# Order and queue of two kinds of loads in the last stage of an FNet and GEGLU kernel

## The chip, the core and the metric

The kernel runs on one core of a Trainium2 chip. The core has a matrix engine (TensorE, PE in the profile), a vector engine (VectorE, DVE), a scalar engine (ScalarE, ACT), a general engine (GpSimd, POOL) and an engine that mostly issues transfers (SyncE, SP). The engines run side by side, each through its own instructions in order, and wait for each other by semaphores. SBUF is the on-chip memory of 128 partitions, PSUM the small memory that TensorE adds into, and the large memory outside is called DRAM in the code. Transfers between DRAM and SBUF are DMAs. SyncE, ScalarE and GpSimd can issue them; each has a queue of its own, and the 16 DMA engines serve all queues.

The metric is device time in microseconds of one execution. Lower is better.

## The reference

`x` has 2048 rows of 448. It is layer-normalised to `xn`. One branch takes the real part of a two-dimensional discrete Fourier transform, with matrices given as inputs; the other is a gated feed-forward network:

```python
a = xn @ hid_re.T;  b = xn @ hid_im.T              # 2048 x 448 each
s = seq_re @ a - seq_im @ b                        # 2048 x 2048 times 2048 x 448
g = silu((gelu(xn @ w_gate) * (xn @ w_up)) @ w_down)
out = x + s * g
```

## The kernel before

All numbers are float32. TensorE works on a rounded form of them (`fp32r`, one pass); where more precision is needed a number is split into a high part, which is the rounded value, and a low part, which is the rest. ScalarE writes the high part and VectorE subtracts it from the number to get the low part (`split`, lines 118 to 120: line 119 is ScalarE's copy, line 120 VectorE's subtraction).

The kernel first computes the feed-forward branch (until about 410 us), then `a` and `b` (`hid_mm`, until about 491 us), and last the product with the 2048 x 2048 matrices, which this change touches. In the last stage the 16 blocks of 128 output rows are taken two at a time: eight rounds, `j` = 0 to 7. The 16 blocks `k` of the inner dimension are taken one after the other. Fourteen of them (`KS`) go through a scheme in the manner of Strassen's multiplication, with seven products where plain multiplication has eight (`seven`); the other two (`KP`) are multiplied plainly, once for each of the two row blocks ("t0" and "t1", `plain`). A round so has 16 units. TensorE takes some 2.2 us for each.

For every one of the fourteen blocks there is a **row tile**: `a` and `b` of that block in seven combinations (blocks 0 to 6 of 448 columns, in which 224 high numbers are followed by their 224 low parts). In the order of `PRODUCTS`, a unit's seven products read the blocks 0, 5, 2, 3, 4, 6 and 1 of its row tile. A product is two matmuls: line 975 multiplies the high part of a coefficient piece with the whole block, line 978 its low part with the block's high half.

Fourteen row tiles do not all fit into SBUF. Ten stay there (`KR`). Of the four others (blocks 0, 1, 4 and 5) two at a time are in the tiles `ts_u0` and `ts_u1`; all four are written once to DRAM (`td`, line 844, by GpSimd). A round begins with the two that are there, goes through the ten, and ends with the two others, which by then have been loaded over the first two; the next round begins with these (`order`). These are the **kept row tiles**. Their loads (line 1042) are four DMAs a tile, each a quarter of the 3136 columns, 392 KB, issued by SyncE at the units 2 to 9 of a round (in the last round at 2, 2, 3 and so on to 8). They are used at the units 12 and 13, the last of the fourteen. In the last round the units 12 and 13 run together, each product for both tiles.

Each unit also needs its **coefficient piece**: combinations of four 128 x 128 blocks of the two matrices. Two DMAs bring it (`load_c`, lines 870 to 882): 192 KB of `ct`, which is input data (line 881), and 128 KB of `sums`, which the kernel has put together earlier in DRAM by an adding DMA (line 882). The plain units load 256 KB of `cp` instead (line 879). Five places hold pieces (`raw_at`; by turns parts of `raw`, `f` and, in the first round, `cc`). VectorE makes two more combinations from both halves of the piece (`sum_c`, lines 888 and 889), then the piece is split into high and low parts (`prep_c`). Both are written into the unit's four slots in turn.

The order of the work is written out by hand: while unit m of TensorE is issued, the combinations of unit m + 4 are made, unit m + 3 is split, and the load of unit m + 8 is issued into the place that m + 3 leaves. At the end of a round VectorE adds up the seven products from PSUM (`gather`, lines 998 to 1006), then in the next round multiplies by the other branch (loaded at line 961) and GpSimd adds `x` with an adding DMA (`give`, lines 1009 to 1019; line 1015). SyncE stores the result (line 1017).

In the built program the DMAs of SyncE use eight completion semaphores in turn, and a DMA waits until the one that used its semaphore before has landed. GpSimd's DMAs have eight of their own.

Of the kernel before, what the change touches and what calls it, by code (L numbers as in the profile page):

```python
# [8 lines left out]
F32 = mybir.dt.float32  # L9
# [4 lines left out]
P = 128  # L14
S = 2048
D = 448
# [15 lines left out]
KX = ((4, 5), (0, 1))  # L32
KP = (10, 15)
KS = sorted(KR + KX[0] + KX[1])
# [11 lines left out]
def fnet_geglu(ctx: ExitStack, tc: tile.TileContext, x, ca, ct, cp, et, wgu, wd, out):  # L46
# [13 lines left out]
    nc = tc.nc  # L60
# [37 lines left out]
    def bank(i, name):  # L98
        return psum.tile([P, 512], F32, name=name, tag=f"b{i}")
# [321 lines left out]
    with tc.manual_schedule():  # L421
# [201 lines left out]
        sums = [dram.tile([P, NS, 2 * P], F32, name=f"sums{j}") for j in range(NK // 2)]  # L623
# [119 lines left out]
        td = {k: dram.tile([P, 7 * D], F32, name=f"td{k}") for k in KX[0] + KX[1]}  # L743
# [8 lines left out]
        T7 = 7 * D  # L752
# [35 lines left out]
        TS, ab, behind = {}, {}, []  # L788
# [64 lines left out]
        def raw_at(m):  # L853
            if m in (4, 5, 9, 10):
                return cc[:, 896 * ((m + 1) % 5) :][:, :896]
            i = (2, 0, 1, 2, 0, 0, 0, 1, 2)[m] if m < 9 else (m - 11) % 5
            return a_r[:, 896 * i :][:, :896] if i < 3 else new["d0"][:, 896 * (i - 3) :][:, :896]
# [12 lines left out]
        def load_c(m):  # L870
            v = raw_at(m)
            if m >= len(units):

                if m < len(units) + 2:
                    nc.sync.dma_start(v[:, :D], xv[:, NK - 2 + m - len(units), :D])
                return
            j, k = units[m]
            if isinstance(k, str):
                nc.sync.dma_start(v[:, : 4 * P], cp[2 * j + int(k[1])])
            else:  # L880
                nc.sync.dma_start(v[:, : 3 * P], ct[j, :, KS.index(k)])
                nc.sync.dma_start(v[:, 4 * P : 6 * P], sums[j][:, KS.index(k)])

        def sum_c(m):

            if m < len(units) and not isinstance(units[m][1], str):
                _, cr1, ci1, s2, s1, _, s4 = [raw_at(m)[:, i * P : (i + 1) * P] for i in range(7)]
                nc.vector.tensor_add(s2, cr1, s1)  # L888
                nc.vector.tensor_add(s4, s2, ci1)  # L889
# [3 lines left out]
        def prep_c(m):  # L893

            if m >= len(units):
                return
            n = (4 if isinstance(units[m][1], str) else 7) * P
            h, l = [v[:, :n] for v in slot_at(m)]
            split(h, l, raw_at(m)[:, :n])
            c_hl[m] = h, l  # L900
            n = nxt.get(m, m + 5)
            if n:
                load_c(n)

        for k in [*range(14), 15, 14]:
# [26 lines left out]
            if k == 8:  # L932
                load_c(0)
# [3 lines left out]
            if k == 12:  # L937
                load_c(1)
                load_c(2)
                sum_c(3)  # L940
# [18 lines left out]
        def load_gx(j, t):  # L959
            if 2 * j + t < NK:  # L960
                nc.sync.dma_start(gx[t], gv[:, 2 * j + t])
# [2 lines left out]
        LOAD_AT = 2  # L964
        STORE_AT = 5, 8
        GX_AT = 11, 12
        PRODUCTS = {1: (1, 0), 6: (3, 5), 2: (2, 2), 7: (5, 3), 5: (4, 4), 3: (6, 6), 4: (0, 1)}

        def seven(m, ps, n=1):

            for q, (i, b) in PRODUCTS.items():
                for u in range(m, m + n):
                    v = TS[units[u][1]][:, b * D : (b + 1) * D]
                    h, l = [w[:, i * P : (i + 1) * P] for w in c_hl[u]]
                    nc.tensor.matmul(  # L975
                        ps[q][:, :D], h, v, start=u % UN == 0, stop=False, skip_group_check=True
                    )
                    nc.tensor.matmul(  # L978
                        ps[q][:, :HD], l, v[:, :HD],
                        start=False, stop=u % UN == NS - 1, skip_group_check=True,  # L980
                    )

        def plain(m, py):
            h, l = c_hl.pop(m)
            for i, k in enumerate(KP):
                for r in range(2):
                    vh, vl = ab[k][r]
                    o = (2 * i + r) * P
                    a, b = h[:, o : o + P], l[:, o : o + P]
                    nc.tensor.matmul(py[:, :D], a, vh, start=i + r == 0, stop=False)  # L990
                    nc.tensor.matmul(py[:, :D], a, vl, start=False, stop=False)
                    nc.tensor.matmul(py[:, :D], b, vh, start=False, stop=i + r == 2)
# [30 lines left out]
        for m, (j, k) in enumerate(units):  # L1023
            u = m % UN
            if u == 0:
                ps = {q: bank(banks[i], f"p{q}_{j}") for i, q in enumerate(PRODUCTS)}
            if u < NS:
                if j < NK // 2 - 1 or u < NS - 2:
                    seven(m, ps)
                elif u == NS - 2:  # L1030

                    seven(m, ps, 2)

                over = 8 if j < NK // 2 - 1 else 7
                for i in range(8):
                    if u != LOAD_AT + i * over // 8:
                        continue
                    i, h = divmod(i, 4)
                    TS[KX[(j + 1) % 2][i]] = TS[KX[j % 2][i]]
                    n, w = KX[(j + 1) % 2][i], T7 // 4  # L1040
                    part_ = slice(h * w, (h + 1) * w)
                    nc.sync.dma_start(TS[n][:, part_].bitcast(F32), td[n][:, part_])
            else:
                py = bank(banks[7 if u == NS else 0], f"py{u - NS}_{j}")
                plain(m, py)
            if u in GX_AT:
                load_gx(j, GX_AT.index(u))

            if u == NS + 1 and m < len(units) - 1:
                todo.pop()()  # L1050
            if m:
                sum_c(m + 4)
            if u == NS - 2 and j == NK // 2 - 1:
                prep_c(m + 3)
                todo = gather(ps)
                todo.insert(6, lambda: nc.vector.tensor_add(cs[0][0], cs[0][0], cs[0][1]))
                for f in todo:
                    f()
            elif u == NS - 1 and j == NK // 2 - 1:
                pass  # L1060
            elif u == NS - 1:
                todo = gather(ps)
                for f in todo[:3]:
                    f()
                prep_c(m + 3)
            elif u == NS:
                for f in todo[3:] if j < NK // 2 - 1 else ():
                    f()
                prep_c(m + 3)
                c = cs[0][0]  # L1070
                todo = [lambda c=c, py=py: nc.vector.tensor_add(c, c, py[:, :D])]
            elif m == len(units) - 1:
                x_ = [raw_at(m + 1 + t)[:, :D] for t in range(2)]
                y = raw_at(m + 3)[:, :D]
                c1, c0 = cs[1][0], cs[0][0]
                nc.vector.tensor_add(c1, c1, cs[1][1])
                todo.pop()()
                for c, t in ((c1, 1), (c0, 0)):
                    nc.vector.tensor_mul(c, c, gx[t])
                for c, t in ((c1, 1), (c0, 0)):  # L1080
                    nc.vector.tensor_add(c, c, x_[t])
                nc.sync.dma_start(ov[:, NK - 2], c0)
                halves = slice(0, HD), slice(HD, D)
                for e in halves:
                    nc.vector.tensor_mul(y[:, e], gx[1][:, e], py[:, e])
                for e, eng in zip(halves, (nc.sync, nc.scalar)):
                    nc.vector.tensor_add(c1[:, e], c1[:, e], y[:, e])
                    eng.dma_start(ov[:, NK - 1, e], c1[:, e])
            elif u == NS + 1:
                prep_c(m + 3)  # L1090
                c = cs[1][0]
                spare = give(j, 0)
                spare.append(lambda c=c, py=py: nc.vector.tensor_add(c, c, py[:, :D]))
                spare += give(j, 1)
                banks = banks[1:] + banks[:1]
            else:
                if m:
                    prep_c(m + 3)
                if m == 4:
                    sums14()  # L1100
                if m == 6:
                    hid_split(14)()
                    load_c(14)
                    load_c(15)
                if spare:
                    spare.pop(0)()
                if u in STORE_AT and stores:
                    stores.pop(0)()
# [57 lines left out]
```

## Time and profile before

| | us |
|---|---|
| median of 3 runs | 786.89 (786.73 to 787.07) |
| profiled execution, its own time | 785.82 |
| its span, first to last instruction | 783.9 |
| TensorE busy in the span | 774.9 (99%) |
| VectorE busy | 593.7 (76%) |
| ScalarE busy | 308.9 (39%) |
| GpSimd busy | 51.8 (7%) |

The profile is of one execution. Rows in order of time show the start in us from the beginning of the span, the duration in us, the engine (SPq is SyncE's DMA issue), the line of the kernel, the operation and the tiles (written <- read, numbers left out). A bracket at the end shows how long the engine was idle before and what ended this. Starts of TensorE's matmuls follow each other closer than their durations, since they are pipelined. Rows of stretches of time show the stretch, its length, the busy time of PE, PEld (TensorE's weight loads), DVE, ACT and POOL with their counts, then TensorE's granted clock, the DMA engines' busy share and GB/s. Rows of waits show who waited for whom: the total in us, how often, and the longest. Rows of groups show count, busy time, mean ns of one, and the idle time before them. Rows of DMA issues show the tiles, the queue, the count, KB each and the median us from issue to landing.

### The profile page before, as it was taken

The page shows a single profiled execution, that of the slowest core. Times are in us where ns is not written, and L with a number is a line of the kernel's source. Part 1 is how long each engine was busy: PE and PEld are TensorE (multiplying, and loading weights), DVE is VectorE, ACT ScalarE, POOL GpSimd, SP SyncE. Part 2 cuts the span into 40 slices and gives each one's busy share as a digit, 9 for nine tenths or more (in the row PEclk, how much of TensorE's full clock was granted, in tenths as well). Part 3 has the DMA queues.
Part 4 walks back from the last instruction along what each step waited for, and adds up shares of the span by engine and source line. Part 5 has one row for each costly group of instructions (what it writes and reads, how often), then busy time and mean ns, then how long its engine had stood idle before and what let it go on. Part 6 is the DMA issues. An engine that isn't in the chain of part 4 may idle for free.

```text
span 783.9 us, 11188 instructions
## 1 busy us (share of the span) xinstructions
PE 774.9 (99%) x4092; PEld 695.4 (89%) x4092; DVE 593.7 (76%) x1045; ACT 308.9 (39%) x430; POOL 51.8 (7%) x82
## 2 busy tenths in 40 slices
PE   9999999999999999999999999999999999999997
PEld 7888888888888888888889999999999999999996
DVE  7877876767766776776675676888888796969686
ACT  3874432331332322322232864544343444444341
POOL 1000211110110010100000000000000000000000
PEclk9999999999999999999999999999999999999999
DMA  8000575353292360546101651778796959697794
GB/s 319 25 3 25 167 220 117 121 121 117 48 258 55 121 135 10 161 131 158 34 13 52 254 229 51 239 256 277 245 318 212 350 172 367 198 322 231 279 278 166
DMA packets 62007, 134.37 MB, mean 171 GB/s; under 512 B 6784, under 2 KB 43520, under 8 KB 61056
## 3 DMA queue, kind: packets, MB, share of 16 engines
q1 hardware_dynamic: 56912, 109.22, 39.7%
q0 software_dynamic: 4896, 24.32, 14.2%
q8 instruction: 32, 0.52, 0.3%
q14 instruction: 23, 0.19, 0.1%
q10 hardware_dynamic: 144, 0.11, 0.0%
HBM read 119.87 MB, written 43.12 MB: 208 GB/s over the span
## 4 chain that ended last, share of the span: by engine, by line
PE 73%; DMA 12%; DVE 10%; issue 2%; SPq 1%; ACT 0%; DVEq 0%
PE x L346 23%; PE po L326 17%; PE ab L803 9%; PE p L975 8%; PE x L354 6%; PE p L978 4%; PE gu L276 4%; DMA ts_u<-td 3%; DMA out<-cc 3%; DVE xt L120 3%; DVE w L120 2%; DMA f<-sums 2%; DMA raw<-sums 2%; DMA raw<-ct 1%; DMA raw<-wgu 1%
## 5 line engine op out<-in xcount | busy, mean ns | idle before, releaser
L326 PE MATMUL po<-wd,hs 128*128 128x448 f32 x672 | 153.0, 366 | 0.0
L326 PEld LDWEIGHTS po<-wd,hs 128*128 128x128 f32 x672 | 125.7, 188 | 14.4
L346 PE MATMUL x<-xt,w 128*128 128x512 f32 x504 | 135.0, 391 | 0.0
L346 PEld LDWEIGHTS x<-xt,w 128*128 128x128 f32 x504 | 94.6, 188 | 16.9
L335 DVE TENSOR_TENSOR gacc<-gacc,po 128x448 f32<-128x448 f32 x96 | 59.1, 618 | 60.9 <-PE po L326 60.9
L119 ACT ACTIVATE w<-raw 128x896 fp32r<-128x896 f32 (+1 forms) x61 | 55.3, 908 | 72.6 <-DVE raw L889 33.7
L346 PE MATMUL x<-thl,w 128*128 128x512 f32 x288 | 77.5, 391 | 0.3 <-DVE tmp L406 0.3
L803 PE MATMUL ab<-w,xt 128*128 128x448 f32 x256 | 68.0, 365 | 0.0
L346 PEld LDWEIGHTS x<-thl,w 128*128 128x128 f32 x288 | 54.0, 188 | 11.6 <-DVE tmp L406 0.7
L354 PE MATMUL x<-xt,w 128*128 128x512 f32 x192 | 59.2, 390 | 0.0
L975 PE MATMUL p<-xt,w 128*128 128x448 f32 x168 | 54.1, 374 | 0.0
L401 ACT ACTIVATE hs<-tmp 128x512 fp32r<-128x512 f32 x24 | 15.2, 634 | 95.3 <-DVE tmp L399 95.3
L803 PEld LDWEIGHTS ab<-w,xt 128*128 128x128 f32 x256 | 48.1, 188 | 3.8
L386 ACT ACTIVATE tmp<-x 128x512 f32<-128x512 f32 x24 | 14.4, 599 | 89.4 <-PE x L354 89.4
L119 ACT ACTIVATE w<-f 128x896 fp32r<-128x896 f32 (+1 forms) x34 | 30.3, 891 | 48.0 <-DVE f L889 26.8
L120 DVE TENSOR_TENSOR w<-raw,w 128x896 fp32r<-128x896 f32 (+1 forms) x41 | 43.0, 1048 | 4.1 <-ACT w L119 3.6
L354 PEld LDWEIGHTS x<-xt,w 128*128 128x128 f32 x192 | 36.0, 188 | 7.7
L975 PE MATMUL p<-ts_u,w 128*128 128x448 f32 x112 | 37.3, 379 | 1.7 <-DMA ts_u<-td 0.7
L975 PE MATMUL p<-ts_u,ts_tmp 128*128 128x448 f32 x112 | 36.5, 374 | 0.0
L888 DVE TENSOR_TENSOR raw<-raw 128x128 f32<-128x128 f32 x69 | 19.9, 288 | 21.2 <-DMA raw<-sums 21.2
L975 PE MATMUL p<-hs,w 128*128 128x448 f32 x112 | 35.6, 374 | 0.0
L803 PE MATMUL ab<-wd,xt 128*128 128x448 f32 x96 | 35.1, 365 | 0.0
(234 smaller groups left out, 1600.0 us busy)
## 6 DMA issues: line engine op xcount, KB each, us to landing
ts_u<-td SPq DMA_DIRECT2D x64, 392.0 KB, 5.9
sums<-ca SPq DMA_DIRECT2D x16, 896.0 KB, 7.5
sums<-ca POOLq DMA_DIRECT2D x16, 896.0 KB, 9.5
raw<-ct SPq DMA_DIRECT2D x69, 192.0 KB, 4.5
raw<-sums SPq DMA_DIRECT2D x69, 128.0 KB, 4.5
f<-ct SPq DMA_DIRECT2D x39, 192.0 KB, 4.4
raw<-wgu SPq DMA_DIRECT2D x14, 512.0 KB, 4.2
td<-ts_u POOLq DMA_DIRECT2D x4, 1568.0 KB, 6.6
```

Source lines behind the costliest of these rows:

```text
L119: nc.scalar.activation(h, src, AF.Copy)
L120: nc.vector.tensor_sub(l, src, h)
L276: nc.tensor.matmul(ps[:, cols], a, xt[:, k, cols], start=n == 0, stop=n == len(mm) - 1)
L326: nc.tensor.matmul(po[:, :D], hs[:, a, kk * P : (kk + 1) * P], wdn[:, b, i], start=n == 0, stop=n == 5,)
L335: nc.vector.tensor_add(ga, ga, po[:, :D])
L346: nc.tensor.matmul(ps, a[i], b[j], start=first and n == 0, stop=n == 2, skip_group_check=True)
L354: nc.tensor.matmul(ps, w["k3" + "gu"[g]][0], xt[:, 3], start=False, stop=True, skip_group_check=True)
L401: nc.scalar.activation(hs[:, 0], g1, AF.Copy)
L803: nc.tensor.matmul(p[:, :D], a, b, start=n == 0, stop=n == len(mm) - 1)
L888: nc.vector.tensor_add(s2, cr1, s1)
L975: nc.tensor.matmul(ps[q][:, :D], h, v, start=u % UN == 0, stop=False, skip_group_check=True)
L978: nc.tensor.matmul(ps[q][:, :HD], l, v[:, :HD], start=False, stop=u % UN == NS - 1, skip_group_check=True,)
```

## The change

Two things change, both in the loads of the last stage.

First, the four parts in which a kept row tile is loaded are no longer quarters of its columns. They are blocks 0 and 5, blocks 2 and 3, blocks 4 and 6, and block 1: the order in which the products of a unit read them. Three parts have two blocks (448 KB), the last has one (224 KB). They are issued by SyncE at the same units as before.

Second, the `sums` half of each coefficient piece is issued by GpSimd and no longer by SyncE. These are 112 DMAs of 128 KB. The `ct` half stays with SyncE.

```diff
@@ load_c
                 nc.sync.dma_start(v[:, : 3 * P], ct[j, :, KS.index(k)])
-                nc.sync.dma_start(v[:, 4 * P : 6 * P], sums[j][:, KS.index(k)])
+                nc.gpsimd.dma_start(v[:, 4 * P : 6 * P], sums[j][:, KS.index(k)])
@@ last stage
+        PARTS = slice(0, 6, 5), slice(2, 4), slice(4, 7, 2), slice(1, 2)
         PRODUCTS = {1: (1, 0), 6: (3, 5), 2: (2, 2), 7: (5, 3), 5: (4, 4), 3: (6, 6), 4: (0, 1)}
@@ in the loop over the units
                     TS[KX[(j + 1) % 2][i]] = TS[KX[j % 2][i]]
-                    n, w = KX[(j + 1) % 2][i], T7 // 4
-                    part_ = slice(h * w, (h + 1) * w)
-                    nc.sync.dma_start(TS[n][:, part_].bitcast(F32), td[n][:, part_])
+                    n = KX[(j + 1) % 2][i]
+                    a, b = [v.rearrange("p (b d) -> p b d", d=D) for v in (TS[n], td[n])]
+                    a, b = a[:, PARTS[h]], b[:, PARTS[h]]
+                    nc.sync.dma_start(a.bitcast(F32), b)
```

## The prediction

> **What bounds the kernel now.** I read the page's first part, then the busy time by stretch, then TensorE's instructions in order of time at the places where it was idle, and last the issues and landings of the DMAs ahead of those places.
>
> ```profile
> PE 774.9 (99%) x4092; PEld 695.4 (89%) x4092; DVE 593.7 (76%) x1045; ACT 308.9 (39%) x430; POOL 51.8 (7%) x82
> ```
>
> TensorE is the bound: 774.9 of 783.9 us. A change that leaves its instructions alone can only remove idle time or add some. The diff touches loads of the last stage alone, so only that stage's idle time is at stake. Five rounds of the last stage (a round is 16 units, about 36 us) give this sum over their stretches:
>
> ```profile
> sum 180.00, PE 178.66 PEld 168.63 DVE 148.21 ACT 75.48 POOL 8.78; mean PE 35.73 PEld 33.73 DVE 29.64 ACT 15.10 POOL 1.76
> ```
>
> So 1.34 us of 180 are idle, one gap in each round. The last of these five, and the gap of the round after it, in order of time (start, duration, engine, line):
>
> ```profile
> 735.08 0.37 PE L975 MATMUL p<-ts_u,w 128*128 128x448 f32 x1
> 735.29 0.26 PE L978 MATMUL p<-ts_u,w 128*128 128x224 f32 x1
> 736.00 0.44 PE L975 MATMUL p<-ts_u,w 128*128 128x448 f32 x1 [0.45 <-DMA f<-sums]
> 736.28 0.27 PE L978 MATMUL p<-ts_u,w 128*128 128x224 f32 x1
> 736.38 0.38 PE L975 MATMUL p<-ts_u,w 128*128 128x448 f32 x1
> ...
> 769.97 0.27 PE L978 MATMUL p<-ts_u,xt 128*128 128x224 f32 x1
> 770.60 0.44 PE L975 MATMUL p<-ts_u,w 128*128 128x448 f32 x1 [0.36 <-DMA ts_u<-td]
> 770.88 0.27 PE L978 MATMUL p<-ts_u,w 128*128 128x224 f32 x1
> ```
>
> A product is a pair L975, L978; undisturbed, starts follow each other by 0.21 us (735.08 to 735.29) and 0.10 us (736.28 to 736.38), 0.31 us a product. The gap at 736.00 comes between the first and the second product of unit 13, on the second kept row tile (`ts_u`). The first product reads its block 0, the second its block 5. Before, the tile comes in four equal quarters of 784 columns, 1.75 blocks each; block 5 (columns 2240 to 2687) ends in the fourth. So TensorE waits for the last quarter when it has used only the first. At 770.60, where the last round runs both kept tiles together, the place is again the first use of the second tile's block 5. The name "f<-sums" in the bracket is the profile's guess from a shared semaphore; neither matmul reads that buffer.
>
> A gap costs more than its bracket. From 735.29 to 736.28 there lie 0.99 us where 0.31 are normal: 0.68 lost, with 0.45 in the bracket. From 769.97 to 770.88 there are 0.91, so 0.60 lost, with 0.36 in the bracket. That is 0.235 over the bracket each time (emptying and refilling the pipeline).
>
> Why the fourth quarter is late is in SyncE's issues and in the DMA load:
>
> ```profile
> 725.25 0.42 SPq L1042 DMA_DIRECT2D ts_u<-td  x1
> ...
> 730.15 0.32 SPq L1042 DMA_DIRECT2D ts_u<-td  x1
> 730.87 0.33 SPq L881 DMA_DIRECT2D raw<-ct  x1
> ```
>
> ```profile
> L1042 SPq DMA_DIRECT2D ts_u<-td x1: 319/319/319, 730.1 to 730.1; - x1
> ...
> DMA to landing us min/median/max: 5.7/5.7/5.7
> ```
>
> ```profile
> 700.00:712.00 12.00, 12.00 (x71) 11.31 (x71) 11.17 (x23) 4.65 (x5) 0.00 (x0) 1.00 0.51 157
> ...
> 724.00:736.00 12.00, 11.55 (x74) 10.80 (x73) 6.74 (x12) 4.55 (x6) 0.00 (x0) 1.00 1.05 372
> ```
>
> The fourth quarter was issued at 730.15 and landed 5.7 later, at 735.9, just before TensorE resumed at 736.00. In the last two columns the DMA share and GB/s: 0.51 and 157 early in the round, 1.05 and 372 from 724 to 736. There the transfers are a full pipe, and what matters is the order of the bytes.
>
> **Part one, the parts in the order of the products.** The bytes are the same (1568 KB a tile), 16 tiles, four DMAs each, at the same units. The parts are now blocks 0 and 5 (448 KB), 2 and 3 (448), 4 and 6 (448), 1 (224). The products use blocks 0, 5, 2, 3, 4, 6, 1, so the second product needs the first part, the fifth the third, and the seventh the fourth. In the round shown, unit 13 starts at 735.08. Its seventh product comes at 735.08 + 6 x 0.31 = 736.94. With the bytes ahead of it unchanged the fourth part lands at 735.9: 1.0 us to spare where it is 0.5 late now. The third part takes the third quarter's place (issued 725.25) but ends 1344 KB into the tile and no longer 1176:
>
> ```profile
> L1042 SPq DMA_DIRECT2D ts_u<-td x1: 420/420/420, 725.3 to 725.3; - x1
> ...
> DMA to landing us min/median/max: 8.2/8.2/8.2
> ```
>
> The third quarter lands at 733.5; 168 KB more at 372 GB/s are 0.45, so 733.9, against the fifth product at 735.08 + 4 x 0.31 = 736.32: 2.4 to spare. In the last round the products of both tiles alternate, so each comes later and the margins are wider. Two parts of each tile are now two pieces of 1792 B a partition where a quarter was one of 3136 B; the stage's idle DMA time early in the round covers it, and in the full stretch I take nothing, with the margin of 1.0 as cover.
>
> All six gaps therefore go: 1.34 from the sum row, 0.36 for the last, and 6 x 0.235 = 1.41 beside the brackets, together 3.1 us. This is also the most that the stage's gaps can give.
>
> **Part two, the sums through GpSimd's queue.** 112 DMAs of 128 KB (one for each unit of coefficients) leave SyncE and go to GpSimd. SyncE saves 112 issues, and its DMAs there wait on earlier DMAs less often:
>
> ```profile
> SPq L882 <- DMA ts_u<-td: 9.6, 16, 1.8
> SPq L1042 <- DMA ts_u<-td: 7.1, 11, 1.7
> ```
>
> Where every eighth DMA of a queue shares a completion semaphore, the built order has SyncE wait for the DMA eight before; without the sums those eight reach further. In a full pipe an earlier issue moves no byte earlier past those ahead of it, so I credit this with nothing.
>
> GpSimd's issue: its plain copies and its adding copies took
>
> ```profile
> L1015 POOL DMA_DIRECT2D cc<-x x14 | 12.3, 882 | 289.2 <-DVE raw L888 137.0 <-DVE raw L889 78.1 <-DVE f L888 68.8
> L844 POOL DMA_DIRECT2D td<-ts_u x4 | 2.2, 557 | 93.9 <-DVE ts_u L842 93.9
> ```
>
> 0.56 to 0.88 us each, so 16 a round cost at most 14 of 36 us on an engine that is idle but for 1.76 us. Behind what do they queue? Behind two `cc<-x` a round, which wait for a VectorE multiply; the next sums in GpSimd's order wait for a later VectorE subtraction anyway, so nothing is held up that was free. The four stores of the kept tiles are out long before. VectorE isn't slowed by GpSimd's descriptor work:
>
> ```profile
> 720.41 0.88 POOL L1015 DMA_DIRECT2D cc<-x  x1 [5.32 <-DVE f L888]
> 720.45 1.09 DVE L120 TENSOR_TENSOR xt<-f,ts_tmp 128x896 fp32r<-128x896 f32 x1
> ...
> 739.05 1.09 DVE L120 TENSOR_TENSOR xt<-raw,ts_tmp 128x896 fp32r<-128x896 f32 x1
> ```
>
> The same subtraction takes 1.09 us beside such an issue and without one.
>
> The unknown is when a plain 128 KB load through GpSimd lands; the trace has none. Rows near it:
>
> ```profile
> raw<-sums SPq DMA_DIRECT2D x69, 128.0 KB, 4.5
> td<-ts_u POOLq DMA_DIRECT2D x4, 1568.0 KB, 6.6
> cc<-x POOLq DMA_DIRECT2D x14, 224.0 KB, 6.2
> ```
>
> From below: today a sums load is issued some 0.4 us behind its `ct` half (an issue of SyncE's takes 0.32 to 0.42 in the rows above), and GpSimd issues beside it, so the pair can land 0.4 earlier. From above: `cc<-x`, which also adds and is nearly twice as large, 6.2 against 4.5, 1.7 later. Nearest is the plain store: 1568 KB at 372 GB/s are 4.2 of its 6.6 us, 2.4 fixed; a sums load at today's median, less 0.3 for its bytes, has 4.2, but this includes queueing in the full pipe, which falls on either queue. I take no shift of the pair, within -0.4 to +1.7.
>
> What would a shift d cost? VectorE waits for the halves already, in the full stretch:
>
> ```profile
> DVE raw L888 <- DMA raw<-sums: 21.2, 20, 2.2
> DVE f L888 <- DMA f<-sums: 12.2, 8, 2.2
> ```
>
> After the last of these waits VectorE works through the gather and the splits without idling, and what it prepares reaches TensorE with least to spare at the next round's unit 1. In two rounds, its subtraction and the first matmul that reads it:
>
> ```profile
> 634.57 1.08 DVE L120 TENSOR_TENSOR w<-f,w 128x896 fp32r<-128x896 f32 x1
> ...
> 742.71 1.08 DVE L120 TENSOR_TENSOR w<-raw,w 128x896 fp32r<-128x896 f32 x1
> ```
>
> ```profile
> 636.86 0.27 PE L978 MATMUL p<-ts_u,w 128*128 128x224 f32 x1
> ...
> 745.22 0.26 PE L978 MATMUL p<-ts_u,w 128*128 128x224 f32 x1
> ```
>
> The first ends at 635.65 (634.57 + 1.08) and is used at 636.86, 1.21 later; the second ends at 743.79 and is used at 745.22, 1.43 later. With its gap gone TensorE arrives some 0.6 earlier, so about 0.7 stays. Up to d = 0.7 part two costs nothing; this is what is late next. Beyond it each of the seven round changes stalls for d - 0.7.
>
> **The sum.** -3.1 + 0 = -3.1 us. The profiled execution took 785.82 (span 783.9 and 1.9 around it), so 782.7; the median of the three runs is 786.89, 1.07 above it, so 783.8 in runs like those. 0.2% of it, about what a measurement of this kernel can tell from no change, is 1.6 us: faster means below 785.3, slower above 788.5.
>
> **Rivals.** First, the gaps stay: the fourth part lands more than 1.0 later than now, or another part misses its product. Against it: 1.0 and 2.4 us to spare. For it: the sums may pass the tile's parts, being no longer behind them in SyncE's order; each passes 128 KB, 0.34 us at 372 GB/s, and three would use up 1.0. If all gaps stay the time is 786.9; if half of the 3.1 stays, 785.3.
>
> Second, slower: the sums land late through GpSimd and VectorE, and behind it TensorE, stalls at unit 1 of each next round. At the upper end, d = 1.7, this costs 7 x (1.7 - 0.7) = 7.0, less the 3.1 of the gaps: 3.9 more, 790.8. It decides from 7 x (d - 0.7) = 3.1, d = 1.15. For it: VectorE waits 33 us for these loads now. Against it: in the full pipe an adding DMA of GpSimd's kept its place by time of issue:
>
> ```profile
> L1015 POOL DMA_DIRECT2D cc<-x x1: 876/876/876, 720.4 to 720.4; - x1
> ...
> DMA to landing us min/median/max: 6.2/6.2/6.2
> ```
>
> ```profile
> L881 SPq DMA_DIRECT2D f<-ct x1: 333/333/333, 721.6 to 721.6; - x1
> ...
> DMA to landing us min/median/max: 5.3/5.3/5.3
> ```
>
> Issued at 720.4 it landed at 726.6; SyncE's load issued at 721.6 landed at 726.9. If that is the rule, a sums load that is issued with its `ct` half lands with it, and d is near 0.
>
> The Trainium skill ("DMA: Bandwidth & Descriptors", section "Queues, rings and completion order") says otherwise: each DMA engine takes turns between the queues that have work, packet by packet. By this the sums of later units would pass the `ct` half that VectorE waits for; two of them shift it by an estimated 0.7, all that is to spare at unit 1, and the sum would still be -3.1, or a few tenths less. The landing order above doesn't show such turns. That is why the slower rival keeps a chance above the rows' own.
>
> **How the numbers follow.** Forecast 0.70, the gaps gone and nothing in their place but some tenths: 783.8. Gaps stay, wholly or by half: 0.15, from 785.3 to 786.9. Slower: 0.15, from 788.5 up. Low is 783.1: 0.2 for the spread of the runs (0.17 about their median), and 0.5 because the 0.235 is read at two of the six gaps (0.32 would give 0.5 more). High is 787.0, which takes in the rival in which all gaps stay. Left out is the slower rival and some 0.05 below the low end. Faster 0.70, same 0.15, slower 0.15, for the same cases. The likeliest case's own range is 783.1 to 785.2.
>
> **What would show it.** Right: no idle TensorE at the second product of unit 13 in any round, and the bytes of 724 to 736 at the same rate. VectorE's waits for the sums stay near 33 us, and its subtraction for unit 1 ends about 0.7 before its use. GpSimd issues 112 loads of sums beside its 14 `cc<-x`, each in 0.5 to 0.9 us. Wrong: TensorE idle at unit 1 or 2 of a round behind VectorE, with sums landing more than 0.7 later than their `ct` halves; or idle still in unit 13, at another product.

## The result, and the profile after

The change made the kernel a little slower: the median of 22 runs is 788.38 us, against 786.37 in 22 runs of the kernel before, taken beside them. The ratio is 1.0024, with an interval of 1.0014 to 1.0034. The forecast was 783.8. The runs of the changed kernel also lie further apart, 783.58 to 790.80 against 785.18 to 787.28. The profiled execution took 787.74 (span 785.9), 1.9 more than that of before.

Line numbers up to 966 stay as they were. In the last stage those of before move by two or three: 975 is now 977 and 978 is 980 (the two matmuls of a product), 1042 is 1045 (the loads of the kept row tiles). Line 1071, now 1074, matters below: it is VectorE's addition of the first plain result ("t0", tile `py`), which reads that result's PSUM bank and so frees it.

The busy times, from the first part of the page of the changed kernel. GpSimd had 51.8 before; the rest stands still:

```profile
PE 774.6 (99%) x4092; PEld 695.2 (88%) x4092; DVE 593.7 (76%) x1045; ACT 308.3 (39%) x430; POOL 113.8 (14%) x194
```

The idle time at the second product of unit 13 has gone. TensorE waits elsewhere. The waits of TensorE between 490 and 790 us, and then of its weight loads (PEld), of the changed kernel:

```profile
PE p L977 <- DVE cc L1074: 2.1, 3, 1.0
PE p L977 <- DMA ts_u<-td: 0.6, 1, 0.6
```

```profile
PEld p L977 <- DVE cc L1074: 3.6, 5, 1.2
```

Of the matmuls' waits one is left for a tile's part; the others are for line 1074, as most of the weight loads' are. This is the start of the last round of the changed kernel, TensorE's rows and then VectorE's:

```profile
745.15 0.38 PE L977 MATMUL p<-ts_u,ts_tmp 128*128 128x448 f32 x1
745.36 0.27 PE L980 MATMUL p<-ts_u,xt 128*128 128x224 f32 x1
746.49 0.47 PE L977 MATMUL p<-ts_u,ts_tmp 128*128 128x448 f32 x1 [0.87 <-DVE cc L1074]
```

```profile
744.83 1.08 DVE L120 TENSOR_TENSOR w<-raw,w 128x896 fp32r<-128x896 f32 x1
745.83 0.61 DVE L1074 TENSOR_TENSOR cc<-cc,py 128x448 f32<-128x448 f32 x1
```

The matmul at 746.49 is the seventh product of unit 0. Its PSUM bank is the one that held `py` of the round just ended, because the list of banks is turned by one place each round (`banks = banks[1:] + banks[:1]`, and "t0" uses `banks[7]`). VectorE frees it at 745.83 + 0.61 = 746.44. In VectorE's order this addition stands behind the gather and behind one subtraction of the split (line 120), so it is late whenever VectorE is. In the same place before, with the rows of VectorE and of TensorE:

```profile
743.71 0.61 DVE L1071 TENSOR_TENSOR cc<-cc,py 128x448 f32<-128x448 f32 x1
```

```profile
744.69 0.38 PE L975 MATMUL p<-ts_u,ts_tmp 128*128 128x448 f32 x1
```

The bank was free at 744.32, and the seventh product came at 744.69. The spare was 0.37, and the gap ahead of it in unit 13 had been 0.68. Take the gap away and TensorE comes 0.3 too early. In rounds 1 to 6 this spare was 0.1 to 0.4 us (subtraction of the same two rows in each round, counting from the round that ends).

How much the last stage loses at each place can be read from the starts of successive matmuls: a product's step is 0.313 us, and what a step has beyond it is lost. "At unit 13" and "at unit 0" add this up over the seven round changes; "last pair" is units 12 and 13 of the last round, which run together; the stage runs from its first matmul to the end of its last. At unit 0 nearly all is lost at the seventh product. The losses of a row are what its stage takes more than those of the last two rows. The kernels e1, e2, e5 and e8 are explained below.

| us | at unit 13 | at unit 0 | last pair | stage |
|---|---|---|---|---|
| before | 2.7 | 0.1 | 0.6 | 288.38 |
| after | 0.9 | 3.7 | 0 | 289.69 |
| order of parts alone (e1) | 0 | 2.8 | 0 | 287.87 |
| queue alone (e2) | 4.8 | 1.0 | 0 | 290.88 |
| parts, loads two units earlier (e5) | 0 | 0 | 0 | 285.04 |
| before, loads two units earlier (e8) | 0 | 0 | 0 | 285.04 |

Of the 1.9 us between the two profiled executions 1.3 lie in this stage; the rest is behind its last matmul.

VectorE waits longer than before, when its waits for `sums` were 21.2 and 12.2. The waits of VectorE from 490 to 790 us in the changed kernel:

```profile
DVE raw L888 <- DMA raw<-ct: 18.3, 12, 2.8
DVE f L888 <- DMA f<-ct: 7.3, 6, 2.4
DVE f L888 <- DMA f<-sums: 5.9, 6, 1.5
DVE raw L888 <- DMA raw<-sums: 5.6, 7, 2.4
```

That is 37.1 in place of 33.4, and most of it, 25.6, is now for the `ct` half, which no part of the change touches. Three rows of the DMA issues of the changed kernel (KB each, and the median us from issue to landing):

```profile
raw<-sums POOLq DMA_DIRECT2D x69, 128.0 KB, 5.2
f<-ct SPq DMA_DIRECT2D x39, 192.0 KB, 5.4
f<-sums POOLq DMA_DIRECT2D x39, 128.0 KB, 5.2
```

Before, `f<-sums` took 4.1 and `f<-ct` 4.4: in this place both halves have become about 1 us slower. `raw<-sums` took 4.5, and `raw<-ct` 4.5 both before and after.

### The profile page after: what moved, and what is told of

Same layout as the page of the kernel before. It is cut to its first block, busy times and chain, and to the rows that moved or that the text cites. A ratio compares the mean times of both kernels' runs of the same rounds, so it can differ in the third digit from the quotient of the medians.

```text
span 785.9 us, 11278 instructions
## 1 busy us (share of the span) xinstructions
PE 774.6 (99%) x4092; PEld 695.2 (88%) x4092; DVE 593.7 (76%) x1045; ACT 308.3 (39%) x430; POOL 113.8 (14%) x194
## 4 chain that ended last, share of the span: by engine, by line
PE 83%; DVE 8%; DMA 5%; issue 2%; SPq 0%; ACT 0%; DVEq 0%
PE x L346 23%; PE po L326 17%; PE p L977 15%; PE ab L803 9%; PE p L980 7%; PE x L354 5%; PE gu L276 4%; DMA ts_u<-td 2%; DVE xt L120 2%; DVE w L120 2%; DMA f<-ct 1%; DMA raw<-wgu 1%; DMA raw<-ct 1%; PE pt L164 1%; PE py L992 1%
## 5 line engine op out<-in xcount | busy, mean ns | idle before, releaser
L346 PEld LDWEIGHTS x<-thl,w 128*128 128x128 f32 x288 | 54.0, 188 | 11.6 <-DVE tmp L406 0.7
L882 POOL DMA_DIRECT2D raw<-sums x69 | 37.9, 550 | 159.3 <-DVE xt L120 43.9
L235 POOL TENSOR_TENSOR raw<-raw 128x128 f32<-128x128 f32 x10 | 5.4, 544 | 276.7 <-DMA raw<-wgu 276.7
```

What stands on the lines that cost most here:

```text
L346: nc.tensor.matmul(ps, a[i], b[j], start=first and n == 0, stop=n == 2, skip_group_check=True)
L882: nc.gpsimd.dma_start(v[:, 4 * P : 6 * P], sums[j][:, KS.index(k)])
```

## The experiments

Each ratio is to executions of the kernel before that were timed beside it.

### Each part alone

The first kernel has the order of parts and leaves the sums with SyncE. In the kernel after:

```diff
-                nc.gpsimd.dma_start(v[:, 4 * P : 6 * P], sums[j][:, KS.index(k)])
+                nc.sync.dma_start(v[:, 4 * P : 6 * P], sums[j][:, KS.index(k)])
```

> Part one alone: the parts in the order of the products, all sums issued by SyncE as before. Bank theory (VectorE's add of the first plain result frees the PSUM bank of the next round's seventh product, with only 0.1 to 0.4 us to spare before): TensorE's gaps in unit 13 go (3.3 us in all), but in five rounds part of it comes back as a stall at unit 0 of the next round, each as long as the old gap less the old spare (0.04, 0.48, 0.15, 0.29, 0.30 us, 1.3 in all): 2.0 us faster, 0.25%. Rival, the theory of the prediction (0.7 to spare at unit 1, nothing tighter): no stall at unit 0, 3.1 us faster, 0.4%.

Measured: 787.03 (785.61 to 787.94), ratio 0.9998 (0.9989 to 1.0006). That is no change, where the bank theory had 2.0 us less and its rival 3.1. No gap is left in unit 13 of any round, yet 2.8 us are lost at unit 0, twice what the bank theory had. TensorE's and VectorE's rows of this kernel, at the start of the last round:

```profile
744.49 0.27 PE L980 MATMUL p<-ts_u,xt 128*128 128x224 f32 x1
745.40 0.47 PE L977 MATMUL p<-ts_u,ts_tmp 128*128 128x448 f32 x1 [0.65 <-DVE cc L1074]
```

```profile
743.74 1.08 DVE L120 TENSOR_TENSOR w<-raw,w 128x896 fp32r<-128x896 f32 x1
744.74 0.61 DVE L1074 TENSOR_TENSOR cc<-cc,py 128x448 f32<-128x448 f32 x1
```

The step that should bring the gain did what it was to do, and the next wait took nearly all of it back.

The second kernel has the queue alone. In the kernel before:

```diff
-                nc.sync.dma_start(v[:, 4 * P : 6 * P], sums[j][:, KS.index(k)])
+                nc.gpsimd.dma_start(v[:, 4 * P : 6 * P], sums[j][:, KS.index(k)])
```

> Part two alone: quarters as before, sums through GpSimd. Turn theory (the DMA engines take turns between the two queues, so sums of later units pass the ct halves and the kept tiles, which land up to 1.5 us later): the gaps in unit 13 grow from 0.1 to 0.7 to about 0.5 to 2.5 us each, since the second product waits for the last quarter: 3 to 8 us slower, 0.4 to 1.0%. Rival (transfers keep their order of issue, no shift): no change, within 0.1%.

Measured: 791.07 (788.53 to 792.47), ratio 1.0044 (1.0029 to 1.0059). So the queue by itself costs some 3.5 us, within what the turn theory had. TensorE's waits from 490 to 790 us, and the last round change's unit 13:

```profile
PE p L975 <- DMA ts_u<-td: 3.3, 4, 1.7
PE p L975 <- DVE cc L1071: 0.5, 2, 0.3
```

```profile
737.34 0.26 PE L978 MATMUL p<-ts_u,w 128*128 128x224 f32 x1
739.31 0.44 PE L975 MATMUL p<-ts_u,w 128*128 128x448 f32 x1 [1.71 <-DMA ts_u<-td]
```

The gaps of before grow from 2.7 to 4.8: the fourth quarter of the tile lands later than before too. With the new order of parts the fourth is wanted by the seventh product and not the second, 1.6 us later (5 x 0.313), which hides most of this in the full change.

### The bank wait taken away

If the bank were the only thing in the way, freeing it earlier would give the whole 3.1 us. In these two kernels VectorE runs the addition right behind the gather, ahead of the split. e3 is e1 with this, e4 the full change with it:

```diff
-            if u == NS + 1 and m < len(units) - 1:
-                todo.pop()()
...
-                prep_c(m + 3)
                 c = cs[0][0]
                 todo = [lambda c=c, py=py: nc.vector.tensor_add(c, c, py[:, :D])]
+                if j < NK // 2 - 1:
+                    todo.pop()()
+                prep_c(m + 3)
```

> Part one, and VectorE's add of the first plain result moved ahead of the split of the next piece, so the PSUM bank is free about 1.1 us earlier. Bank theory: the stalls at unit 0 that part one alone leaves go, and unit 1's spare (1.2 us less the old gap less 0.6) stays at or above zero in nearly all rounds: 3.0 us faster than before, 0.38%, about 1.0 us faster than part one alone. Rival (the bank isn't the wait): the same time as part one alone, within 0.3 us.

> The changed kernel with the same early add. Bank theory: its stalls at unit 0 (0.25, 0.27, 1.32, 0.38, 1.03 us in its profile) shrink by up to 0.6 each, where unit 1's spare then decides: 1.5 to 2.5 us faster than the changed kernel, so level with the kernel before to 0.1% faster. Rival (the loss is elsewhere): as slow as the changed kernel, 0.2 to 0.3% slower than before.

Measured: e3 786.29 (784.39 to 787.21), ratio 0.9989 (0.9981 to 0.9998); e4 787.91 (783.71 to 790.61), ratio 1.0015 (0.9999 to 1.0032). Each ratio is only 0.0009 below that of the same kernel without the edit, less than the intervals can tell apart; the bank theory had 1.0 us for e3 and 1.5 to 2.5 for e4. In the profiled executions e3's stage took 288.34 us and e1's 287.87. In e3 VectorE's rows have changed places, and TensorE waits for the split's low part at unit 1 instead:

```profile
744.48 0.61 DVE L1071 TENSOR_TENSOR cc<-cc,py 128x448 f32<-128x448 f32 x1
745.01 1.08 DVE L120 TENSOR_TENSOR w<-raw,w 128x896 fp32r<-128x896 f32 x1
```

```profile
746.15 0.37 PE L980 MATMUL p<-ts_u,w 128*128 128x224 f32 x1 [0.21 <-DVE w L120]
```

So the bank is only the first of several waits that lie close together, and all of them hang on one thing: when the last coefficient pair of the crowded stretch lands and VectorE can begin. VectorE's combination for unit 1 of the next round starts 1.1 to 1.8 us behind the start of unit 13 before (rounds 1 to 6), 1.0 to 2.1 in e1, 0.9 to 3.2 after. In all three kernels, at every round change, it starts within 0.1 us of the landing of the pair's later half. So this landing, and nothing on VectorE itself, sets the start. A place for a pair is reused only when VectorE has split what is in it, so a late VectorE also issues the next loads late: landing, VectorE and issue follow each other in a ring. TensorE, 99% busy, was waiting for that ring in its slowest stretch.

### The loads of the tiles begun earlier

If that is right, relieving the crowded stretch should remove both kinds of wait. `LOAD_AT` sets the unit of a round at which the first tile part is issued; the eight follow one a unit. Three kernels begin at unit 0: e5 is e1, e7 is the full change, and e8 is the kernel before.

```diff
-        LOAD_AT = 2
+        LOAD_AT = 0
```

> Part one alone, sums on SyncE, and the kept tiles' loads begin at unit 0 of a round in place of unit 2. Loop theory (what sets a round's length in the middle rounds is not TensorE but the loop of pair landing, VectorE, load issue; VectorE waits some 5 us a round for pairs in the full stretch of the pipe, and TensorE's gaps are only where this shows): the pipe's idle time early in the round is used, the last part and the pairs land some 4 us earlier against unit 13, no stall in unit 13, 0 or 1, rounds of 35.6 us: 3 us faster than the kernel before, 0.35 to 0.4%. Rival (the bytes of a round are the limit wherever they lie): the stalls stay as in part one alone, level with the kernel before.

> The changed kernel with the kept tiles' loads begun at unit 0. Loop theory: what part two delays matters only in the full stretch, which now lies earlier by two units: 2.5 to 3.5 us faster than the kernel before, within 0.1% of part one alone with the same start. Rival (GpSimd's queue costs wherever it is used): 0.2% or more behind part one alone with the same start.

> The kernel before, quarters and all sums on SyncE, with the kept tiles' loads begun at unit 0 and nothing else changed. Loop theory: the start alone removes the stalls, since the last quarter lands some 4 us earlier and so before unit 13: 3 us faster, 0.35 to 0.4%, the same as with part one. Rival (the order of the parts is needed): gaps in unit 13 remain, at most 1 us faster.

Measured: e5 782.08 (781.83 to 782.57), ratio 0.9945 (0.9933 to 0.9957); e7 782.88, 0.9955 (0.9942 to 0.9967); e8 782.55, 0.9951 (0.9939 to 0.9962). With 786.07 for the kernel before beside them, the gains are 4.0, 3.2 and 3.5 us, what the loop theory had or a little more. All three beat both kernels, the runs of each lie within 0.8 us, and no time is lost in the stage, which takes 285.03 us in e7 too. The stretch from 560 to 740 us in e1, in e5 and in e8 (its length, then the busy times and counts of PE, PEld, DVE, ACT and POOL, the clock, the DMA engines' share and GB/s):

```profile
560.00:740.00 180.00, 179.05 (x1103) 169.29 (x1102) 148.29 (x285) 75.35 (x85) 8.77 (x10) 1.00 0.83 270
```

```profile
560.00:740.00 180.00, 180.00 (x1112) 171.22 (x1111) 151.55 (x290) 76.30 (x86) 8.77 (x10) 1.00 0.84 273
```

```profile
560.00:740.00 180.00, 180.00 (x1113) 171.22 (x1112) 151.79 (x290) 76.31 (x86) 8.76 (x10) 1.00 0.84 273
```

The DMA share is nearly the same, 0.83 and 0.84; its place in the round is another. Three stretches of 12 us of one round, in e1 and then in e5 (the round begins at 706.9 in e1 and at 704.6 in e5, and the last row reaches into the next):

```profile
710.00:722.00 12.00, 12.00 (x79) 11.46 (x78) 11.79 (x24) 5.87 (x7) 1.74 (x2) 1.00 0.79 227
722.00:734.00 12.00, 12.00 (x79) 11.44 (x78) 8.30 (x15) 4.96 (x7) 0.01 (x1) 1.00 1.06 367
734.00:746.00 12.00, 11.35 (x65) 10.46 (x64) 9.22 (x20) 3.79 (x5) 0.00 (x0) 1.00 0.63 208
```

```profile
708.00:720.00 12.00, 12.00 (x79) 11.47 (x78) 11.49 (x24) 5.67 (x6) 1.75 (x2) 1.00 0.95 293
720.00:732.00 12.00, 12.00 (x79) 11.46 (x78) 7.83 (x15) 5.09 (x6) 0.00 (x0) 1.00 1.06 368
732.00:744.00 12.00, 12.00 (x72) 11.33 (x71) 10.99 (x22) 4.74 (x6) 0.00 (x0) 1.00 0.51 151
```

In both the second row is full, 1.06. In e5 more of the bytes go in the first row, 0.95 against 0.79, and the row behind the full one has 0.51 against 0.63: the crowd is over sooner, and TensorE's last row is 12.00 of 12.00 against 11.35. In e7 and e8 the combination for unit 1 starts 0.2 to 0.8 us ahead of unit 13 at every round change (in e5 too, but for one, 1.1 behind), and the spare at the bank is 0.8 us where it was 0.1 to 0.4. And e8 shows that the new order of parts isn't needed for this: with the quarters of before, begun two units earlier, the gaps in unit 13 are gone as well.

### Other splits between the two queues

If the trouble is that two halves of one pair are in two queues, both halves in GpSimd's should cure it. e6 moves `ct` there too; e9 is e1 with the tiles' parts on GpSimd.

```diff
-                nc.sync.dma_start(v[:, : 3 * P], ct[j, :, KS.index(k)])
+                nc.gpsimd.dma_start(v[:, : 3 * P], ct[j, :, KS.index(k)])
```

> The changed kernel with the ct half through GpSimd as well, so that a pair lies in one queue and SyncE keeps the kept tiles, stores and plain pieces. Turn theory: the pair shares the pipe by turns with SyncE's queue and is no longer behind the tile parts: ct lands before its sums again, VectorE's waits for pairs fall below 20 us, but the last tile part lands later than in the changed kernel, 2 to 4 us after unit 13 starts where 1.9 is free: stalls in unit 13, within 0.3% of the kernel before either way. Rival (transfers keep their order of issue, and the loss is GpSimd's slow issue): pairs land as late as in the changed kernel or later, since GpSimd now issues two DMAs of 0.55 us each: 0.3 to 0.6% slower.

```diff
-                    nc.sync.dma_start(a.bitcast(F32), b)
+                    nc.gpsimd.dma_start(a.bitcast(F32), b)
```

> Part one, with the kept tiles' 64 part loads through GpSimd and all pairs (ct and sums) on SyncE: the other half of the traffic is moved. Loop theory: pairs are no longer behind tile parts in SyncE's queue, so VectorE waits less than the 33 us of the kernel before, while a part that lands up to 1.9 us later than now does no harm: 1 to 3 us faster than the kernel before. Rival (any use of GpSimd's queue beside SyncE's in the full stretch lengthens it): level or slower, with VectorE's waits at 33 us or more.

Measured: e6 794.64 (792.4 to 796.32), ratio 1.0106 (1.0087 to 1.0124); e9 793.44 (791.29 to 794.88), ratio 1.0089 (1.0073 to 1.0104). Both are slower than any other kernel. VectorE's waits for pairs in e6:

```profile
DVE raw L888 <- DMA raw<-sums: 27.7, 20, 3.9
DVE f L888 <- DMA f<-sums: 16.8, 13, 2.8
```

In e6 the halves land in their old order again, as the turn theory had it, but the pair as a whole is late: 44.5 us in these two rows, 33.4 before and less than 20 by that theory. Nothing is lost at unit 13 (0.7 us in the last pair); of the 11.6 us that its stage loses 8.0 lie at unit 0. The rival had the late pairs, and at 0.3 to 0.6% too small a price. Why the pairs are late was not settled. e9 came out as its rival had it: slower, with VectorE's waits for pairs at 37.8 us (25.4 and 12.4), above 33. GpSimd's rows show one thing that its instruction order does, here in round 5:

```profile
682.23 0.88 POOL L1017 DMA_DIRECT2D cc<-x  x1 [21.66 <-DVE raw L888]
683.14 2.03 POOL L1045 DMA_DIRECT2D ts_u<-td  x3
```

Three parts stand behind `cc<-x` (line 1015 before), which waits for VectorE, and come out at once, in rounds 1 to 7 alike. The parts were in time even so: nothing is lost at unit 13, and of the 7.3 us that e9's stage loses 5.7 lie at unit 0, behind late pairs. Whether the pairs are late because three parts come out together or because of the second queue is not shown, and so this run says little about the queues themselves.

### The queue without the crowd

The last two kernels ask what GpSimd's queue costs where the pipe isn't full: e10 is the full change and e11 the kernel before, both without the loads of the kept row tiles.

```diff
-                    nc.sync.dma_start(a.bitcast(F32), b)
```

> The changed kernel without the loads of the kept row tiles (left out; the last two units of a round then use the tiles that are there). Loop theory: the pipe never fills, pairs land 2.5 to 3 us after their issue, no TensorE idle in the stage from unit 3 of the first round on, 3.5 to 4.5 us faster than the kernel before. Rival (sums through GpSimd cost by their issue alone): VectorE still waits over 10 us for sums, and the time is 1 us or more above the next kernel's.

> The kernel before without the loads of the kept row tiles. Loop theory: as the changed kernel without them, within 0.1%, 3.5 to 4.5 us faster than the kernel before with them. Rival: 1 us or more faster than the changed kernel without them.

Measured: e10 783.03 (782.7 to 783.24), ratio 0.9957 (0.9945 to 0.9970); e11 782.62 (782.44 to 782.8), ratio 0.9952 (0.9938 to 0.9966). The DMA issues of e10, its stretch from 560 to 740 us, and the same two of e11:

```profile
raw<-sums POOLq DMA_DIRECT2D x69, 128.0 KB, 2.6
```

```profile
560.00:740.00 180.00, 180.00 (x1112) 171.08 (x1111) 150.80 (x291) 76.28 (x86) 48.01 (x81) 1.00 0.63 183
```

```profile
raw<-sums SPq DMA_DIRECT2D x69, 128.0 KB, 2.4
```

```profile
560.00:740.00 180.00, 180.00 (x1113) 171.06 (x1112) 150.83 (x290) 76.28 (x86) 8.75 (x10) 1.00 0.64 183
```

They are 3.1 and 3.6 us below the 786.17 of the kernel before beside them, a little less in e10 than the 3.5 to 4.5 that the theory had. A load through GpSimd lands 0.2 us later, GpSimd is busy for 39 us more, VectorE waits for no pair, and TensorE never idles in either; the stage takes 285.03 us in both. In a pipe that is 0.63 full the queue gains nothing and costs the rounds nothing. Its price in the full change comes from the crowd; e7, whose stage is as short with the loads only moved, says the same.

### How the queue moves the landings

How does the crowd make the queue cost time? At the pairs of units 9 to 12 SyncE, with one issue less to make, issues the next tile part at once, while GpSimd is still issuing the sums. SyncE's row for the part, and then the rows of the two halves of the pair (ns of the issue, time of the issue, and the time to landing), in the changed kernel:

```profile
680.38 0.47 SPq L1045 DMA_DIRECT2D ts_u<-td  x1
```

```profile
L881 SPq DMA_DIRECT2D f<-ct x1: 328/328/328, 680.0 to 680.0; - x1
...
DMA to landing us min/median/max: 4.5/4.5/4.5
```

```profile
L882 POOL DMA_DIRECT2D f<-sums x1: 566/566/566, 680.4 to 680.4; - x1
...
DMA to landing us min/median/max: 5.6/5.6/5.6
```

`ct` landed at 684.5, the sums at 686.0. That is 1.5 behind, where the pair of the same unit, in another round of the kernel before, had them 0.36 behind (issued 715.37 and 715.75, landed 720.09 and 720.45). The tile's 448 KB landed with the sums, at 686.1. At the turn of the round it is the other way about. A `ct` load of SyncE's, and a later unit's sums of GpSimd's:

```profile
L881 SPq DMA_DIRECT2D raw<-ct x1: 333/333/333, 695.4 to 695.4; - x1
...
DMA to landing us min/median/max: 6.8/6.8/6.8
```

```profile
L882 POOL DMA_DIRECT2D f<-sums x1: 546/546/546, 696.3 to 696.3; - x1
...
DMA to landing us min/median/max: 5.3/5.3/5.3
```

Issued at 695.4 the `ct` half landed at 702.2; the sums of a later unit, issued at 696.3, landed at 701.6. They passed it. VectorE wanted the earlier unit's `ct` first. This is the shift that reaches the round change: from round 1 on the half of unit 1's pair that lands last, and with which VectorE's combination then starts, is `ct`, 0.3 to 3.1 us behind its sums; before it was the sums each time, some 0.35 behind. How much each of the two shifts costs was not measured apart.

## Why the prediction was wrong

**What bounds the kernel, and the gaps.** Six gaps at the second product of unit 13, for the tile's last part, together 3.1 us: right in place, cause and size (2.7 at unit 13 and 0.6 in the last pair, by the table; a seventh gap, of 0.1 in round 1, was not counted). That the order of parts removes them: right, in e1 in every round, though with a smaller margin than the 1.0 forecast (in round 6 the fourth part landed 1.25 us behind the start of unit 13 and was wanted 1.9 behind it); in the full change one stays, 0.9 us in round 6, where the fourth part landed 2.6 us behind the start of unit 13 and was wanted 1.9 behind it.

**The step that failed: "With its gap gone TensorE arrives some 0.6 earlier, so about 0.7 stays."** The spare was read at the wrong consumer. It holds for the subtraction that it was worked out for, but VectorE's addition of `py` stands behind that in order, and the seventh product of unit 0, before unit 1, needs its bank. There the spare was 0.1 to 0.4 us, less than the gaps that were to go. The step also took the gaps for a loss of TensorE's own. The rounds' length was set by the landings of the pairs and by VectorE behind them, and the tile's part was just what came a little later still; e5, e7 and e8 show this, where moving the crowd removes both kinds of wait. With the gaps gone, e1 is level: of the 3.1 us the stage kept 0.5 in the profiled execution, and the runs none that can be told from zero.

**The second: "I take no shift of the pair", and "up to d = 0.7 part two costs nothing".** The range of the shift, -0.4 to 1.7, holds the place shown above (0.36 became 1.5 behind `ct`), but not all: the sums of unit 9 landed 1.6 to 2.5 behind their `ct` in rounds 1 to 7, where 0.3 was usual before. The value taken from the range was wrong, and so was the limit, as the spare of 0.7 was. Two things were missed. SyncE, freed of the sums, sends the tile's part earlier, beside them. And later sums pass an earlier `ct`. e2 prices this at 0.44% without the other part; beside it, the step from e1's ratio of 0.9998 to 1.0024 is some 2 us.

**The slower rival** was the right kind of case, VectorE late at the round change, with a wrong place (the bank at unit 0, not unit 1), a wrong half (VectorE waits 25.6 us for `ct` and 11.5 for the sums) and a higher price than the event (790.8 against 788.38). What speaks for it in the prediction, 33 us of waits for these loads, deserved more weight than the one landing order set against it.

**The landing order.** An adding DMA of GpSimd's, issued 1.2 us ahead of a `ct` load, had landed 0.3 ahead; I read it as "by time of issue". It was one pair, and the adding DMA was first in both, so it couldn't have shown a passing. The rule that the prediction cites of the Trainium skill ("DMA: Bandwidth & Descriptors", section "Queues, rings and completion order"), that the DMA engines take turns between queues, agrees with the landings at 701.6 and 702.2 above: the later load, in a queue of its own, comes first. The same page says in its section "Issuing engines are not separate DMA queues" that issuing from several engines saves only the time of the issue; e10 and e11 agree that there is no more to gain, and e2 shows that in a full pipe there is something to lose.

**The signs it named.** GpSimd's 112 issues at 0.5 to 0.9 us: right, 550 ns in the mean for `raw`. Waits for the pairs near 33: wrong, 37.1. The sign given for a miss, TensorE idle behind VectorE at the next round, came, one unit earlier than named.

**Still open:** the shares of the two shifts in the queue's price, and why both halves through GpSimd (e6), or the tiles' parts (e9), are slower still.

## What to carry to other kernels

An idle gap of the busiest engine is worth only what the next releaser leaves: list for the whole stretch behind the gap everything that the engine will need, PSUM banks included, and take the smallest spare. Where one stretch of a round has its transfers crowded, look first whether some of them can begin in the emptier part: here that gave 0.5% by one constant, and the reordering that treated the symptom gave nothing. Halves of one operand that are wanted together lost their common order here in two queues, and the queue that was relieved sent its next transfer sooner: look for both before moving a load to another queue.

## What was not expected of the hardware

A 128 KB load issued by GpSimd 0.9 us behind a 192 KB load of SyncE's landed 0.6 us ahead of it (701.6 and 702.2), while SyncE's queue still had a tile's parts ahead of that load (the last landed at 700.1). With the tiles' loads left out the same loads took 2.6 us from GpSimd and 2.4 from SyncE, so the queue itself adds little; GpSimd's issue of one took 0.55 us, SyncE's of a `ct` half 0.33. The spread differs too, for what reason was not tested: 22 runs of the changed kernel lie within 7.2 us, six of the same kernel with `LOAD_AT = 0` within 0.8.
